# An output store that waits for an accumulating transfer, and a product split around another, in a convolution and two-matmul kernel

## The chip, the cores and the metric

The kernel runs on one core of a Trainium2 chip. The metric is the device time of one execution in microseconds (us); lower is better. The engines are called PE (TensorE, matmul), PEld (its weight loads), DVE (VectorE), ACT (ScalarE), POOL (GpSimd) and SP (SyncE, which here only issues DMAs). They run side by side, each in its own order, and wait for one another through semaphores.

## The reference

```python
w = weight_gen - max(weight_gen, axis=-1)          # (8, 4096, 8 heads, 7 taps)
w = exp(w);  w = w / (sum(w, axis=-1) + 1e-9)
x_pad = concatenate([zeros(B, 6, D), x], axis=1)   # six rows of zeros ahead of each batch row
x_unf = x_pad[:, arange(S)[:, None] + arange(7)]   # the seven rows that end at a token
y = einsum('bshk,bskhg->bshg', w, x_unf)           # (32768 tokens, 192), 24 channels per head
h = y @ w_in                                       # (192, 2048)
out = (h - tanh(h)) @ w_out                        # (2048, 192), float32
```

A convolution over seven taps whose weights are a softmax of their own for each token and head, and then two matmuls with `h - tanh(h)` between them.

## The kernel before

**Tiling.** The 32768 tokens are worked in 32 superblocks of 1024 tokens, numbered by `n`; each of the 128 partitions holds 8 tokens of a superblock (`J = 8`). A batch row is 4 superblocks long, so superblocks 0, 4, 8, ... begin with six rows of zeros, their halo.

**One superblock, stage by stage.**

1. SP loads `x` into one of four places of `x_ring` (line 172) and, for a superblock that begins a batch row, fills the halo with zeros (line 182). An even superblock's load brings its halo along (1344 KB), an odd one's shares it with the even one before (768 KB). SP also loads the weights `wg_t` (line 161, 224 KB).
2. ACT takes their exponential (line 202), DVE sums and scales it (`wsm`).
3. POOL multiplies `x` with the weights, tap by tap (line 297): taps 0 to 3 into the tile `pa`, taps 4 to 6 into `pb`. `pa` has three buffers, `pb` one. DVE makes one or two of the eight tokens of taps 0 to 2 (`HELP`); its operand stands at line 338.
4. POOL issues two accumulating DMAs (line 286). The three-tap transfer adds `pb` to taps 0 to 2 of `pa` (`first_sum`, in the profile `pa<-pb`, 1152 KB). For superblocks 10 to 31 the two-tap transfer (`second_sum`, `pa<-pa`, 768 KB) then adds taps 2 and 3 to taps 0 and 1, so that two taps are left to be added by PE; superblocks 4 to 9 leave four.
5. PE transposes what is left and adds it up in PSUM (`pc`, line 524), ACT copies it to `convT` (line 550).
6. In 16 steps `f`, PE makes 128 rows of `h` (`ph`, line 584), ACT their tanh (line 597), DVE the difference `gt` (line 598). In between PE runs the second matmul of the superblock before (`obank`, line 653), ACT copies its result to `out_sb` (line 672, two buffers), and SP stores it (line 676, 768 KB).

**Order.** The loop over `n` (its turns are called iterations here) writes out by hand what each step holds, and the order in which instructions are written is the order on each engine's queue. In iteration `n` PE works on the first matmul of superblock `n`. At step 1 the program writes, in this order: POOL's products of taps 0 to 3 of superblock `n + 2`, the two-tap transfer of `n + 1`, the load of `x` for `n + 3` (from iteration 9 on; it waits for the first of those products), and, after the second matmul's share of that step, the store of superblock `n - 2`. At a later step come POOL's product of taps 4 to 6 for `n + 2` and its three-tap transfer (`rest`), at step 8 the zero fill for `n + 3` where there is one, at step 11 the load of `wg_t` for `n + 5`, at steps 13 and 14 the transposes of `n + 1`. POOL and SP work strictly in this order: an instruction that waits holds up all behind it.

**Names that the change touches.** `LAST_TAP` and `FILL`: for the superblocks in `LAST_TAP`, tap 3 (which the three-tap transfer does not touch) is not made together with taps 0 to 2 but in `rest`: the first `FILL[n]` tokens just ahead of the three-tap transfer's issue, the others behind it. `LOCKED` and `LOCK`: for the superblocks in `LOCKED`, `rest` is written at step 10 and the three-tap transfer also waits for DVE's difference of that step. `dma_sum` returns the DMA instruction, `order(inst, other, reason)` makes one instruction wait for another (for a DMA: until it has landed).

Of the kernel before, what the change touches and what calls it, by code (L numbers as in the profile page):

```python
# [16 lines left out]
def kernel(  # L17
# [8 lines left out]
    nc = tc.nc  # L26
# [25 lines left out]
    EXTRA_NORM = False  # L52

    WG_AT = 11
    LOCK, LOCKED = 10, tuple(range(15, 32))
    WARM = 0
    SUM_LATE = ()
    SUM_BEHIND = ()
    HELP = {4: ((2, 3, 2, 1),), 5: ((3, 3, 2, 1),), 6: ((4, 3, 2, 1),), 7: ((5, 3, 2, 1),), 8: ((6, 3, 2, 1), (6, 12, 2, 1)), 9: ((7, 3, 2, 1), (7, 12, 2, 1)), 10: ((8, 3, 2, 1),), 11: ((9, 3, 2, 1),), 12: ((10, 3, 2, 1),), 13: ((11, 3, 2, 1),), 14: ((12, 3, 2),), 15: ((13, 3, 2),), 16: ((14, 3, 2),), 17: ((15, 3, 2),), 18: ((16, 3, 2),), 19: ((17, 3, 2),), 20: ((18, 3, 2),), 21: ((19, 3, 2),), 22: ((20, 3, 2),), 23: ((21, 3, 2),), 24: ((22, 3, 2),), 25: ((23, 3, 2),), 26: ((24, 3, 2),), 27: ((25, 3, 2),), 28: ((26, 3, 2),), 29: ((27, 3, 2),), 30: ((28, 3, 2),), 31: ((29, 3, 2),)}
    CUTS0 = [0, 2, 4]  # L60
    LAST_TAP = (4, 5, 6, 7, 8)
    X_LATE = ()
    ZERO_AT = 8
    PACE, PACED = None, ()
    SCALE_TWICE = True
    RELIEF = ()
    ACT_HELP = {}
    FILL = {4: 2, 5: 2, 6: 2, 7: 2, 8: 2}
    PART_FILL = {2: 1}
    SCALE_EARLY = ()  # L70
    REST2 = None
# [6 lines left out]
    X3_AT = 3  # L78
    X3_BEHIND = None
    HALF = ()  # L80
    WOUT_CAST = ()
    SKEW = 6
    TAPS1 = ((True, 0, 1, 0, 8), (True, 1, 2, 0, 8), (False, 4, 6, 0, 8), (False, 6, 7, 0, 8), (False, 2, 4, 0, 8))
# [56 lines left out]
    tap_of = {}  # L140
    pace_of = {}
    sum_of = {}

    def order(inst, other, reason):
        tc.add_manual_dep(
            inst.ins,
            other.ins.name,
            mybir.DependencyInfo(mybir.DependencyClass.Sync, mybir.DependencyReason.DATA),
            reason=reason,
        )  # L150
# [3 lines left out]
    def tokens(t, n):  # L154

        m = n // 2
        return t[2 * m * TOK : 2 * (m + 1) * TOK].rearrange("(p s j) ... -> p s j ...", p=P, j=J)[:, n % 2]
# [127 lines left out]
    def dma_sum(out, in_):  # L285
        return nc.gpsimd.dma_start(  # L286
            out=out.rearrange("p k j d -> p k (j d)"),
            in_=in_.rearrange("p k j d -> p k (j d)"),
            accum_op=mybir.AluOpType.add,
            max_dma_last_dim=2 * J * D,  # L290
        )
# [19 lines left out]
    def shares(n):  # L311

        top = [J] * KA
        dve, act = [], []
        for a, b, kh, nt in [(*e, 1)[:4] for e in HELP.get(n, ())]:
            dve.append((a, b, kh, top[0] - nt, top[0]))
            top[:kh] = [t - nt for t in top[:kh]]
        for a, b, k in ACT_HELP.get(n, ()):
            top[k] -= 1
            act.append((a, b, k, top[k]))  # L320
        return dve, act, top
# [35 lines left out]
    def products(n, taps=None, sums=None, hooks={}):  # L357
# [24 lines left out]
        def mul(eng, k0, k1, j0=0, j1=J):  # L382
            w = wsm_v if eng is nc.vector else wsm[:]
            return tap_product(eng, prod(k0, k1), x_t, w[:, j0:j1, :, k0:k1], (1, K), k0, k1, j0, j1)

        def parts(*ks):
            return [[prod(k, k + 1)[:, 0] for k in ks]] * NC
# [14 lines left out]

        end = KA - 1 if n in LAST_TAP else KA
        left = shares(n)[2]

        def most(k0, k1):
            return mul(nc.gpsimd, k0, k1, 0, left[k0])
# [7 lines left out]
        for k0, k1 in zip(cuts, cuts[1:]):  # L415
            if n - 1 in SUM2_EARLY and k0 == end - 1:
                second_sum(n - 1)
            m = most(k0, k1)
            if first is None and n - 1 in sum_of:
                sum_of.pop(n - 1)()  # L420
            first = first or m
        x_after[n + 1] = first
        second_sum(n - 1)
        def rest():
            a = PART_FILL.get(n, 0)
# [14 lines left out]
            else:  # L440
# [4 lines left out]

                if n in LAST_TAP and n in SUM_BEHIND:
                    most(KA - 1, KA)
# [3 lines left out]
                else:  # L451
                    a = min(FILL.get(n, 0), left[KA - 1]) if n in LAST_TAP else 0
                    if a:
                        mul(nc.gpsimd, KA - 1, KA, 0, a)
                    first_sum()
                    if n + 1 in SCALE_EARLY:
                        prescale(n + 1)
                    if n in LAST_TAP and a < left[KA - 1]:
                        mul(nc.gpsimd, KA - 1, KA, a, left[KA - 1])
                if n in TWO_SUMS:  # L460
                    to_sum[n] = pa
                    prods_of[n] = parts(0, 1)
                elif n in HALF:
                    to_sum[n] = pa
# [3 lines left out]
                if n == NTOT - 1:  # L468
                    second_sum(n)
                    third_sum(n)  # L470
# [3 lines left out]
    def prescale(n):  # L474

        wsm, wsm_v, e_t, zr = wsm_of[n]
        scale(nc.gpsimd, wsm[:], e_t, zr[:])
        wsm_of[n] = (wsm, wsm_v, None, None)

    def second_sum(n):  # L480

        if n in to_sum:
            pa = to_sum.pop(n)
            pairs = 1 if n in HALF else 2
            dma_sum(pa[:, 0:pairs], pa[:, 2 : 2 + pairs])
            if n in THREE or n in SINGLE:
                whole[n] = pa

# [150 lines left out]
    def out_stream():  # L639

        for i in range(LAST + 1):
            ops = []
            for r, blk in ((0, i), (1, i - 1)):
                if not 0 <= blk < LAST:
                    continue
                n, j = divmod(blk, J)
                if r == 0:
                    half[blk] = obank[blk % 2]
                ops.append((r, n, j, half[blk]))
            for f in range(NFT):  # L650
                for r, n, j, po in ops:
                    col = (j % 2) * HT + (j // 2) * P
                    mm = nc.tensor.matmul(  # L653
                        po[:, 0:D],
                        lhsT=g_of[n][f][r * R : (r + 1) * R, col : col + P],
                        rhs=w_out[r * R : (r + 1) * R, f, :],
                        start=(r == 0 and f == 0),
                        stop=(r == 1 and f == NFT - 1),
                    )
                    if r == 1 and f == 0 and i in (1, LAST):  # L660
                        order(mm, probe[0] if i == 1 else last_act[0], "row tiles in one bank")
                if f == NFT - 1 and i > 0:
                    store_out(i - 1)
                yield

    def store_out(blk):
        n, j = divmod(blk, J)
        po = half.pop(blk)
        if j == 0:
            out_of[n] = opool.tile([P, J, D], FP32, name="out_sb")  # L670
        out_sb = out_of[n]
        last_act[0] = nc.scalar.activation(out=out_sb[:, j, :], in_=po[:, 0:D], func=ACT.Copy)  # L672
        if j == J - 1:
            out_of.pop(n)
            g_of.pop(n)
            nc.sync.dma_start(
                out=tokens(out, n),
                in_=out_sb[:],
            )

    pairs = out_stream()

# [132 lines left out]
    if SOFT_EARLY:  # L815
# [6 lines left out]
        sums=SUMS1,  # L822
        hooks={} if WOUT_CAST else {6: load_w_out},
    )
# [202 lines left out]
```

## Time and profile before

| what | us |
|---|---|
| three runs | 738.18, 738.52, 741.08 (median 738.52) |
| the profiled execution's own time | 740.38 |
| its span in the profile | 738.5 |

| engine | busy us | instructions |
|---|---|---|
| PE | 716.7 | 13472 |
| DVE | 681.1 | 718 |
| POOL | 660.6 | 170 |
| ACT | 636.7 | 871 |

The profile records one execution. The chain of waits is the work that ended last, followed back from the end: at each step to what released it, or to the instruction before it on the same engine. A row of the timeline gives start, duration, engine, line, operation, the tiles, how many were merged, and in brackets how long the engine stood idle just before and what ended that. For DMAs the trace gives the issue on the queue that issues it (SPq, or POOL) and, where something waits for it, the time from issue to landing. Rows by line give count and shortest, median and longest duration in ns, with first and last start in us.

### The profile page before, as it was taken

Reading aid. Unit: us, or ns where it says so; the run is one execution under the profiler, and the core shown is the slowest. Engines: PE = TensorE matmul, PEld = TensorE weight load, DVE = VectorE, ACT = ScalarE, POOL = GpSimd, SP = SyncE. Lnnn points to the kernel's source line nnn. Section 1 sums busy time; section 2 is a strip of 40 time slices with the busy share of each in tenths; the row PEclk is TensorE's granted clock in tenths of the full one; section 3 lists DMA queues with packets and bytes.
Section 4 is the critical chain, followed back from the end, with each engine's and each line's share of the span. In section 5 each row is a group of like instructions: output and inputs, shape, how many; then the busy total and the mean of one; then the engine's idle time right before and its main releaser. Section 6 shows DMA issues by size and latency. Waiting matters only on the chain.

```text
span 738.5 us, 29769 instructions
## 1 busy us (share of the span) xinstructions
PE 716.7 (97%) x13472; PEld 551.1 (75%) x13472; DVE 681.1 (92%) x718; ACT 636.7 (86%) x871; POOL 660.6 (89%) x170
## 2 busy tenths in 40 slices
PE   3799999999998999999999999999999999999998
PEld 2477777777776777777777777777777777777777
DVE  7999999999998899999999999999999999988883
ACT  4888888988887889988989989898998999888882
POOL 7999999999999999989999999999999999996000
PEclk9999999999999999999999999999999999999999
DMA  7745276765558887766987878798786889766312
GB/s 203 163 101 162 101 188 142 184 177 122 136 145 206 199 227 168 175 158 171 233 206 172 191 147 206 179 236 197 157 185 160 207 197 216 172 140 110 88 45 87
DMA packets 35053, 122.97 MB, mean 167 GB/s; under 512 B 4607, under 2 KB 9455, under 8 KB 33006
## 3 DMA queue, kind: packets, MB, share of 16 engines
q0 software_dynamic: 20208, 53.48, 41.7%
q1 hardware_dynamic: 14718, 67.59, 26.1%
q8 instruction: 105, 1.72, 0.9%
q14 instruction: 22, 0.18, 0.1%
HBM read 45.08 MB, written 25.17 MB: 95 GB/s over the span
## 4 chain that ended last, share of the span: by engine, by line
PE 88%; DVE 4%; POOL 4%; DMA 2%; issue 1%; ACT 1%; POOLq 0%; DVEq 0%
PE obank L653 42%; PE ph L584 41%; PE pc L524 4%; POOL pa L297 2%; DVE gt L598 2%; PE po L697 1%; DMA pa<-pa 1%; POOL pb L297 1%; DVE pa L297 1%; DVE pb L297 0%; DMA wg_t<-in_weight_gen_dram 0%; ACT th L597 0%; POOL pa L286 0%; DVE obank L256 0%; DVE zsum L216 0%
## 5 line engine op out<-in xcount | busy, mean ns | idle before, releaser
L598 DVE TENSOR_TENSOR gt<-ph,th 128x1024 bf16<-128x1024 f32 x512 | 598.6, 1218 | 36.5 <-ACT th L597 29.7
L597 ACT ACTIVATE th<-ph 128x1024 f32<-128x1024 f32 x512 | 513.0, 1027 | 67.0 <-PE ph L584 52.8
L584 PE MATMUL ph<-convT,w_in 64*128 64x512 bf16 x3072 | 413.5, 378 | 4.6 <-DVE gt L598 3.6
L653 PEld LDWEIGHTS <-gt 64*128 64x128 bf16 x7936 | 354.0, 94 | 84.3 <-issue 12.4
L653 PE MATMUL obank<-w_out,gt 64*128 64x192 bf16 x7936 | 407.2, 243 | 0.1
L297 POOL TENSOR_TENSOR pa<-x_ring,wsm 128x3072 bf16<-128x3072 f32 (+2 forms) x73 | 346.1, 5008 | 0.2
L297 POOL TENSOR_TENSOR pb<-x_ring,wsm 128x4608 bf16<-128x4608 f32 (+4 forms) x34 | 286.3, 8423 | 2.2 <-DVE wsm L279 1.2
L584 PEld LDWEIGHTS <-w_in 64*128 64x128 bf16 x3072 | 159.8, 94 | 80.1 <-issue 12.8
L672 ACT ACTIVATE out_sb<-obank 128x192 f32<-128x192 f32 x248 | 81.7, 329 | 9.5 <-PE obank L653 8.3
L550 ACT ACTIVATE convT<-pc 128x1024 bf16<-128x1024 f32 (+1 forms) x62 | 50.7, 820 | 5.9 <-PE pc L524 5.6
L286 POOL DMA_DIRECT2D pa<-pa x24 | 39.5, 1648 | 8.3 <-DMA pa<-pb 8.0
L286 POOL DMA_DIRECT2D pa<-pb x28 | 37.3, 1333 | 10.4 <-POOL pb L297 6.7
L524 PEld LDWEIGHTS <-pa 64*128 64x128 bf16 x1920 | 39.2, 100 | 9.3 <-POOL pb L297 3.0
L524 PE MATMUL pc<-ident,pa 64*128 64x64 bf16 x1824 | 38.6, 191 | 4.1 <-DMA pa<-pa 2.5
L216 DVE TENSOR_REDUCE zsum<-wg_t 128x32 f32<-128x224 f32 (+1 forms) x61 | 23.6, 388 | 3.0 <-ACT wg_t L202 3.0
L202 ACT ACTIVATE wg_t<-wg_t 128x448 f32<-128x448 f32 x32 | 18.2, 569 | 6.8 <-DMA wg_t<-in_weight_gen_dram 6.8
L279 DVE TENSOR_TENSOR wsm<-wg_t,pc 128x448 f32<-128x448 f32 x27 | 16.8, 621 | 2.5
L297 DVE TENSOR_TENSOR pa<-x_ring,ph 128x384 bf16<-128x384 f32 x30 | 16.6, 554 | 1.3
L243 DVE RECIPROCAL pc<-zsum 128x64 f32<-128x64 f32 x27 | 14.8, 549 | 0.0
L524 PE MATMUL pc<-ident,pb 64*128 64x64 bf16 x216 | 4.9, 206 | 9.3 <-POOL pb L297 9.3
L524 PEld LDWEIGHTS <-pb 64*128 64x128 bf16 x288 | 6.3, 107 | 9.8 <-POOL pb L297 9.3
L697 PE MATMUL po<-w_out,gt 64*128 64x192 bf16 x256 | 11.9, 243 | 0.0
(26 smaller groups left out, 55.1 us busy)
## 6 DMA issues: line engine op xcount, KB each, us to landing
pa<-pb POOLq DMA_DIRECT2D x28, 1152.0 KB, 9.7
out_dram<-out_sb SPq DMA_DIRECT2D x31, 768.0 KB, 4.1
x_ring<-in_x_dram SPq DMA_DIRECT2D x15, 1344.0 KB, 8.3
pa<-pa POOLq DMA_DIRECT2D x24, 768.0 KB, 8.4
x_ring<-in_x_dram SPq DMA_DIRECT2D x17, 768.0 KB, 5.3
wg_t<-in_weight_gen_dram SPq DMA_DIRECT2D x32, 224.0 KB, 6.0
w_out<-in_moe_w_out_dram POOLq DMA_DIRECT2D x1, 768.0 KB, 9.7
out_dram<-out_sb SPq DMA_DIRECT2D x4, 192.0 KB, 3.5
```

Of the source, the lines that this page charges most:

```text
L202: last_exp[0] = nc.scalar.activation(out=wg_t[:].rearrange("p j h k -> p (j h k)"), in_=wg_t[:].rearrange("p j h k -> p (j h k)"), func=AC ...
L216: nc.vector.reduce_sum(out=zsum_of[n][:, j0 * H : j1 * H], in_=e_of[n][:, j0:j1].rearrange("p j h k -> p (j h) k"), axis=AX.X,)
L286: return nc.gpsimd.dma_start(out=out.rearrange("p k j d -> p k (j d)"), in_=in_.rearrange("p k j d -> p k (j d)"), accum_op=mybir.AluOpTyp ...
L297: return eng.tensor_mul(bass.AP(tensor=out.tensor, offset=out.offset + j0 * D, ap=[out.ap[0], [J * D, nk], [G, run], [1, G]]), bass.AP(ten ...
L524: nc.tensor.matmul(pc[r][:, col : col + R] if home else pc[:, r, col : col + R], lhsT=prods[c][gi][r * R : (r + 1) * R, 2 * j : 2 * j + 2] ...
L550: last_conv[0] = nc.scalar.activation(out=out, in_=pc[:, :, 0:cols].rearrange("p r (cj t) -> p r cj t", t=R), func=ACT.Copy,)
L584: nc.tensor.matmul(ph[:, r, :], lhsT=w_in[r * R : (r + 1) * R, c, ff], rhs=convT[r * R : (r + 1) * R, c, :], start=(c == 0), stop=(c == NC ...
L597: last_act[0] = nc.scalar.activation(out=th[:], in_=ph_f, func=ACT.Tanh)
L598: last_sub[0] = nc.vector.tensor_sub(gt[:], ph_f, th[:])
L653: mm = nc.tensor.matmul(po[:, 0:D], lhsT=g_of[n][f][r * R : (r + 1) * R, col : col + P], rhs=w_out[r * R : (r + 1) * R, f, :], start=(r == ...
L672: last_act[0] = nc.scalar.activation(out=out_sb[:, j, :], in_=po[:, 0:D], func=ACT.Copy)
L697: nc.tensor.matmul(po[:, r, 0:D], lhsT=g_of[n][f][r * R : (r + 1) * R, col : col + P], rhs=w_out[r * R : (r + 1) * R, f, :], start=(f == 0 ...
```

## The change

Three tables grow and one wait is added. Superblock 14 joins `LOCKED`. Superblocks 9 and 10 join `LAST_TAP` and `FILL`, with two tokens ahead of the transfer. And the store of superblock `n` (5 to 30, where superblock `n + 3` has a two-tap transfer that is already written, so 7 to 28) waits until the two-tap transfer of `n + 3` has landed; that transfer is written in the same step just ahead of the store.

```diff
-    LOCK, LOCKED = 10, tuple(range(15, 32))
+    LOCK, LOCKED = 10, tuple(range(14, 32))
...
-    LAST_TAP = (4, 5, 6, 7, 8)
+    LAST_TAP = (4, 5, 6, 7, 8, 9, 10)
...
-    FILL = {4: 2, 5: 2, 6: 2, 7: 2, 8: 2}
+    FILL = {4: 2, 5: 2, 6: 2, 7: 2, 8: 2, 9: 2, 10: 2}
...
+    STORE_BEHIND = tuple(range(5, 31))
...
+    second = {}
...
             pa = to_sum.pop(n)
             pairs = 1 if n in HALF else 2
-            dma_sum(pa[:, 0:pairs], pa[:, 2 : 2 + pairs])
+            second[n] = dma_sum(pa[:, 0:pairs], pa[:, 2 : 2 + pairs])
...
-            nc.sync.dma_start(
+            dma = nc.sync.dma_start(
                 out=tokens(out, n),
                 in_=out_sb[:],
             )
+            if n in STORE_BEHIND and n + 3 in second:
+                order(dma, second[n + 3], "order of the transfers")
```

Each engine runs the same instructions in the same order as before, except that on POOL, for superblocks 9 and 10, one product of 128x3072 becomes three of 128x1536, 128x384 and 128x1152; the last of them stands behind the three-tap transfer.

## The prediction

> I write F1(n) for the three-tap transfer of superblock n (line 286, `pa<-pb`) and S2(n) for its two-tap transfer (`pa<-pa`).
>
> **What bounds the kernel now.** I read the page first, then busy time by superblock, then the chain of waits, then single lines around the one place that stood out.
>
> ```profile
> PE 716.7 (97%) x13472; PEld 551.1 (75%) x13472; DVE 681.1 (92%) x718; ACT 636.7 (86%) x871; POOL 660.6 (89%) x170
> ```
>
> TensorE is busy 97%. An average hides where the other 3% lie, so I cut the span at superblocks (columns: window, length, busy time of PE, PEld, DVE, ACT, POOL, granted clock, DMA share, GB/s):
>
> ```profile
> 177.00:199.50 22.50, 22.50 (x450) 17.20 (x448) 21.54 (x25) 19.92 (x28) 22.20 (x6) 1.00 0.63 166
> 222.50:248.10 25.60, 23.08 (x397) 17.62 (x394) 20.44 (x23) 19.53 (x28) 25.30 (x6) 0.93 0.89 212
> 270.05:291.82 21.77, 21.77 (x402) 16.77 (x400) 20.85 (x23) 19.65 (x28) 21.47 (x6) 1.00 0.80 197
> 235.60:238.55 2.95, 0.43 (x31) 0.44 (x30) 2.34 (x3) 1.02 (x1) 2.65 (x3) 1.00 0.14 40
> 238.55:241.95 3.40, 3.40 (x49) 2.69 (x43) 0.00 (x0) 1.49 (x2) 3.40 (x2) 0.50 0.83 145
> ```
>
> Before iteration 9 a superblock takes 22.50 us with TensorE full (450 matmuls); after it 21.77, full again (402). There only less matmul work would help. Iteration 9 alone takes 25.60, of which 3.83 (25.60 - 21.77) is loss: TensorE stands, and then has half its clock for 3.40 us. All that this change can win is in that window. The chain, in order of time (start, us, what), says who is late:
>
> ```profile
> 192.76 0.57 DVE pa L297
> 193.33 0.03 POOLq L286
> ...
> 217.10 9.48 POOL pa L297 x2
> ...
> 227.11 10.90 DMA pa<-pa
> ```
>
> S2(10) was issued by POOL at 227.11, after products of its own, and took 10.90. The row of the matmuls that waited for it (the transposes of superblock 10, `pc`), and POOL's and SP's rows around it, from the timeline:
>
> ```profile
> 238.14 0.74 PE L524 MATMUL pc<-ident,pa 64*128 64x64 bf16 x32 [2.52 <-DMA pa<-pa]
> ...
> 110.56 1.76 POOL L286 DMA_DIRECT2D pa<-pb  x1
> 130.92 1.76 POOL L286 DMA_DIRECT2D pa<-pb  x1
> 174.30 2.71 POOL L297 TENSOR_TENSOR pa<-x_ring,wsm 128x1152 bf16<-128x1152 f32 x1
> 180.70 6.09 POOL L297 TENSOR_TENSOR pa<-x_ring,wsm 128x3072 bf16<-128x3072 f32 x1
> 186.28 8.80 POOL L297 TENSOR_TENSOR pb<-x_ring,wsm 128x4608 bf16<-128x4608 f32 x1
> 195.38 1.29 POOL L286 DMA_DIRECT2D pa<-pb  x1 [0.30 <-POOL pb L297]
> 215.82 1.28 POOL L286 DMA_DIRECT2D pa<-pb  x1 [0.30 <-POOL pb L297]
> 227.11 1.72 POOL L286 DMA_DIRECT2D pa<-pa  x1
> 237.50 1.28 POOL L286 DMA_DIRECT2D pa<-pb  x1 [0.30 <-POOL pb L297]
> 238.32 11.01 POOL L297 TENSOR_TENSOR pa<-x_ring,wsm 128x2688 bf16<-128x2688 f32 x2
> 248.79 1.72 POOL L286 DMA_DIRECT2D pa<-pa  x1
> 270.47 1.72 POOL L286 DMA_DIRECT2D pa<-pa  x1
> 326.33 1.28 POOL L286 DMA_DIRECT2D pa<-pb  x1 [2.39 <-DVE gt L598]
> ...
> 222.10 0.33 SPq L172 DMA_DIRECT2D x_ring<-in_x_dram  x1
> 222.53 1.25 SPq L676 DMA_DIRECT2D out_dram<-out_sb  x1
> 232.07 0.70 SPq L182 DMA_DIRECT2D x_ring<-zero  x1
> 232.87 0.62 SPq L161 DMA_DIRECT2D wg_t<-in_weight_gen_dram  x1
> ```
>
> The stall is 2.52, so TensorE wanted S2(10) at 235.62 (238.14 - 2.52). The rest of the 3.83, 1.31, is the halved clock.
>
> [...]
>
> **Tap 3 split for 9 and 10 (FILL, LAST_TAP).** Taps 2 and 3 (128x3072, 5.58 from 180.70 to 186.28) become 128x1536, 128x384 and, behind F1, 128x1152. Superblocks that already do this show F1 to F1 in 20.36 (110.56 to 130.92), those that do not 20.44 (195.38 to 215.82): the pieces cost nothing, because the 384 runs in the 0.30 that F1 waits for `pb` anyway. F1(9) would be ready at 180.70 + 2.8 (half of 5.58) + 9.1 (186.28 to 195.38) = 192.6; but VectorE's help product for 9 releases line 286 only at 193.36 (193.33 + 0.03 in the chain), so F1(9) goes at 193.4, 2.0 early. F1(10) follows at 213.3 to 213.8 (20.36, or less by the 0.5 that POOL idled). Then S2(10) = F1(10) + 11.29 (215.82 to 227.11) + the 1152 left over (2.7 by its row, some 0.5 of it under its neighbours, as 6.09 is 5.58 from start to start for the larger product) = 226.8 to 227.8. Before: 227.11. All of POOL's work still stands ahead of S2(10), so this part alone is worth -0.3 to +0.7; I take 0. What it does buy is that F1(10) leaves the DMA engines 2 us sooner.
>
> **The store behind S2.** In SP's order stand: load of x(12), store of block 7, zero fill of x(12)'s halo, load of wg. The store (768 KB) now goes only once S2(10) has landed. What S2 takes in other company:
>
> ```profile
> L286 POOL DMA_DIRECT2D pa<-pa x1: 1722/1722/1722, 270.5 to 270.5; - x1
> ...
> DMA to landing us min/median/max: 8.8/8.8/8.8
> L286 POOL DMA_DIRECT2D pa<-pa x1: 1715/1715/1715, 248.8 to 248.8; - x1
> ...
> DMA to landing us min/median/max: 8.3/8.3/8.3
> L286 POOL DMA_DIRECT2D pa<-pa x1: 1213/1213/1213, 684.0 to 684.0; - x1
> ...
> DMA to landing us min/median/max: 7.0/7.0/7.0
> ```
>
> With no load of x beside it 7.0 (S2(31)); with the large load of x, and a store issued just before it, 8.8 (S2(12)); here 10.9 with the store 4.6 ahead of it (222.53). No row has the large load without a store. Bounds 7.0 and 10.9; I take 8.0, below 8.8 because store, zero fill and wg (232.87, inside S2's time) all go. S2(10) then lands at 227.1 + 8.0 = 235.1, 0.5 before TensorE wants it. Stall and halved clock go: -3.83, less 0.2 for a rest of the stall: **-3.6**.
>
> What is queued behind the store pays for it. The zero fill now comes after it, and POOL's first product of superblock 12 (238.32, that is S2 + 11.2) needs it. Its own landing no row shows; the nearest is the store's:
>
> ```profile
> wg_t<-in_weight_gen_dram SPq DMA_DIRECT2D x32, 224.0 KB, 6.0
> pa<-pb POOLq DMA_DIRECT2D x28, 1152.0 KB, 9.7
> ...
> L676 SPq DMA_DIRECT2D out_dram<-out_sb x31: 332/344/1272, 66.4 to 725.3; - x31
> ...
> DMA to landing us min/median/max: 3.4/4.1/7.6
> ```
>
> The store is issued at S2 + 8.1 and alone lands in 3.4. A zero fill that ends with it is in place at S2 + 11.5: POOL waits 0.3. If it first begins when the store has landed, and takes another 3.4, POOL waits 3.7. Below, 0. I take 0.3, since it is issued 0.4 after the store and is 4.5 KB. It happens for superblocks 12, 16, 20, 24 and 28.
>
> [...]
>
> Does TensorE feel a late POOL? It wants S2(11) one superblock after 235.62, at 257.4. S2(11) is issued at 248.8 + 0.3 and, with the smaller load of x and no store, takes at most 8.3: lands at 257.4, more likely 256.6. From there POOL repeats in 21.68 (248.79 to 270.47) against TensorE's 21.77, and is 2.39 ahead of its lock at 326.33. So waits of 0.3 every fourth superblock (POOL regains 4 x 0.09 between) stay covered.
>
> The wg load would go at 235.1 + 0.1 + 0.4 + 0.7 = 236.3 and land at 242.3 (6.0); its exponential on ScalarE ran at 247.3, 243.5 after the gain. Covered by 1.2 here, more later.
>
> ```profile
> L202 ACT ACTIVATE wg_t<-wg_t x1: 570/570/570, 247.3 to 247.3; 128x448 f32<-128x448 f32 x1
> ```
>
> If wg were late, ScalarE would stand in line with its tanh behind it. The output buffer comes around only after two superblocks: a store 8 us later costs nothing. F1 goes 10.4 after S2 (227.11 to 237.50) and meets the store's last 1.1; it has 11.29 against its 9.7: covered by 1.6.
>
> **Lock for 14.** F1(14) now waits for VectorE's subtraction at step 10 of iteration 12, one superblock before the 326.3 of F1(15): 304.5, and 300.9 after the gain. POOL comes to F1(14) at about 302.6 (237.50 + 3 x 21.68), later: no wait, 0.
>
> **Sum.** -3.6 against the profiled execution's 740.38 (span 738.5 and 1.9 around it) gives 736.8. The median of the three runs, 738.52, lies 1.86 lower, so **734.9** for the median. The three runs spread by 2.9, about what this stall with its clock is worth, so runs may have had it in part.
>
> **Rivals.**
> A. S2(10) stays a little late (9.5 instead of 8.0): stall 1.0, clock perhaps kept. Gain 2.5: 736.0. For it: 8.8 was with a store only just ahead.
> B. The change does nothing: another stream (the large x load) held S2(10), which still lands at 10.9; the stall stays at 2.5, and FILL gives -0.3 to +0.7: 738.5. For it: S2(12) beside the large load takes no less than 8.8. Against: DMA share falls to 0.14 while TensorE waits, after 16 us of transfers close together that the store was part of.
> C. The zero fill takes the store's place as the wait, five times. At 2.0 each, less the 0.36 regained: 5 x 2.0 - 4 x 0.36 = 8.6 of delay in POOL. TensorE absorbs what POOL is ahead: 2.4 at the lock, and about 1.5 from faster transfers. 8.6 - 3.9 - 3.6 = +1.1: 739.6; at 2.6 each +4.1: 742.6. It turns the sign from about 1.8 each. Against: in 3.4 us even the whole store is through.
> D. The store, now released just ahead of every F1, makes F1 longer than the 11.29 that S2 leaves it. At 12.5 POOL waits 1.2 for some 20 superblocks, 24, less 3.9 and 3.6: 755. Against: only 1.1 of overlap.
>
> **How the numbers follow.** Forecast 0.55, A 0.15, B 0.08, C 0.17, D 0.05. The likeliest gives 734.9. Half a per cent, about what a measurement of this kernel can tell from no change, is 3.7 us: below 734.8 is faster, above 742.2 slower. The forecast lies on that edge: of its 0.55 I give 0.38 to faster and 0.17 to same; A goes to same but for 0.02; B to same; C is half same, half slower; D slower. Faster 0.40, same 0.46, slower 0.14. The low end, 733.8, is the whole 3.83 and a runs' scatter of about 0.9; the high end, 739.8, takes in A, B and the milder half of C. Forecast's own range: 733.8 to 736.0.
>
> **What would show it.** The step from 222.50 on takes 21.8 to 22.5 and not 25.6, with the clock at 1.00 and no wait of `pc` for `pa<-pa`. S2(10) is issued within 0.7 of 227.1 and lands in 8.5 or less. The store of block 7 is issued at 234 to 236 instead of 222.53. F1(9) goes at 193.4. POOL's product for 12 shows a wait under 0.5 for a transfer. I am wrong if S2(10) still lands after 235.6, if POOL waits over 1.5 for the zero fill, or if F1 lands later than 11.3 after its issue.

## The result and the profile after

| | runs | median us | lowest to highest |
|---|---|---|---|
| before | 15 | 738.97 | 737.75 to 741.23 |
| changed | 15 | 737.07 | 735.85 to 740.14 |

The ratio is 0.9974 with a 95% interval of 0.9963 to 0.9986: faster by 1.9 us (0.26%), where 3.6 had been forecast. The profiled execution of the changed kernel took 736.08 (span 734.2), against 740.38 (span 738.5) before: 4.3 us less. So one pair of profiles shows more than the forecast, and the medians show half of it. The profile of before lies 1.4 above its median of 738.97, that of the changed kernel 1.0 below its own. The experiments had to explain that difference.

The shares of the chain of waits by engine in the kernel before, then the engines' busy times and the same shares in the changed kernel:

```profile
PE 88%; DVE 4%; POOL 4%; DMA 2%; issue 1%; ACT 1%; POOLq 0%; DVEq 0%
...
PE 714.7 (97%) x13472; PEld 549.7 (75%) x13472; DVE 681.0 (93%) x718; ACT 636.4 (87%) x871; POOL 661.0 (90%) x174
...
PE 94%; DVE 4%; ACT 0%; DMA 0%; issue 0%; DVEq 0%
```

TensorE now holds 94% of the chain instead of 88%, and POOL is no longer in it. Busy time of iteration 9 in the changed kernel, first cut at its new length and then at the length it had before (columns as in the prediction):

```profile
222.50:244.30 21.80, 21.80 (x407) 16.85 (x403) 20.91 (x23) 19.68 (x28) 21.50 (x7) 1.00 0.74 186
222.50:248.10 25.60, 25.60 (x480) 20.06 (x476) 24.63 (x29) 23.16 (x32) 25.30 (x7) 1.00 0.78 195
```

The superblock takes 21.8 with TensorE full, and the clock stays at 1.00. In the 25.60 us in which before 397 matmuls ran, 480 run. The timeline of the changed kernel around that place: TensorE's transposes of superblock 10, POOL from F1(9) on, and SP:

```profile
235.55 0.65 PE L526 MATMUL pc<-ident,pa 64*128 64x64 bf16 x32
...
193.97 1.29 POOL L288 DMA_DIRECT2D pa<-pb  x1 [0.81 <-POOL pa L299]
213.85 1.76 POOL L288 DMA_DIRECT2D pa<-pb  x1
227.32 2.19 POOL L288 DMA_DIRECT2D pa<-pa  x1
228.10 9.79 POOL L299 TENSOR_TENSOR pb<-x_ring,wsm 128x4608 bf16<-128x4608 f32 x1
238.19 1.28 POOL L288 DMA_DIRECT2D pa<-pb  x1 [0.30 <-DMA x_ring<-zero]
...
222.79 0.33 SPq L174 DMA_DIRECT2D x_ring<-in_x_dram  x1
234.86 0.34 SPq L678 DMA_DIRECT2D out_dram<-out_sb  x1
235.29 0.70 SPq L184 DMA_DIRECT2D x_ring<-zero  x1
236.10 0.91 SPq L163 DMA_DIRECT2D wg_t<-in_weight_gen_dram  x1
```

The transposes begin at 235.55 with no wait in brackets. S2(10) is issued at 227.32 (before: 227.11); the store of block 7 has gone from 222.53 to 234.86, which is when S2(10) has landed. The two-tap transfers of superblocks 10 and 12 by themselves:

```profile
L288 POOL DMA_DIRECT2D pa<-pa x1: 2195/2195/2195, 227.3 to 227.3; - x1
...
DMA to landing us min/median/max: 7.5/7.5/7.5
...
L288 POOL DMA_DIRECT2D pa<-pa x1: 1717/1717/1717, 271.2 to 271.2; - x1
...
DMA to landing us min/median/max: 7.3/7.3/7.3
```

S2(10) takes 7.5 instead of 10.9, S2(12) 7.3 instead of 8.8. The packets in the traces show what gave way: before, the store's packets (6144 bytes each) ran from 228.7 to 234.3, among those of S2(10), the last of which ended at 237.7; in the changed kernel S2(10)'s ended at 234.5 and the store's began at 235.7. The signs that the prediction named for this place came, but for F1(9), which went at 193.97 and not at 193.4.

### The profile page after: what moved, and what is told of

It is laid out like the page before. It is cut to its first block, busy times and chain, and to the rows that moved or that the text cites. A ratio compares the mean times of both kernels' runs of the same rounds, so it can differ in the third digit from the quotient of the medians.

```text
span 734.2 us, 29779 instructions
## 1 busy us (share of the span) xinstructions
PE 714.7 (97%) x13472; PEld 549.7 (75%) x13472; DVE 681.0 (93%) x718; ACT 636.4 (87%) x871; POOL 661.0 (90%) x174
## 3 DMA queue, kind: packets, MB, share of 16 engines
q8 instruction: 105, 1.72, 0.9%
## 4 chain that ended last, share of the span: by engine, by line
PE 94%; DVE 4%; ACT 0%; DMA 0%; issue 0%; DVEq 0%
PE obank L655 45%; PE ph L586 44%; PE pc L526 4%; DVE gt L600 2%; PE po L701 1%; DVE pa L299 1%; DVE pb L299 0%; DMA wg_t<-in_weight_gen_dram 0%; DVE obank L258 0%; DVE zsum L218 0%; DVE wsm L281 0%; ACT th L599 0%; ACT wg_t L204 0%; DVE obank L281 0%; ACT convT L544 0%
```

## The experiments

All ratios are against the kernel before, run on the same chip.

| kernel | runs | median us | ratio | 95% interval |
|---|---|---|---|---|
| before again | 12 | 739.27 | 1.0009 | 0.9997 to 1.0022 |
| changed again | 5 | 736.30 | 0.9969 | 0.9957 to 0.9981 |
| store's wait alone | 7 | 736.68 | 0.9963 | 0.9946 to 0.9981 |
| tap 3's split alone | 11 | 739.09 | 1.0006 | 0.9997 to 1.0014 |
| lock of 14 alone | 12 | 739.17 | 0.9998 | 0.9988 to 1.0008 |
| only block 7's store waits | 11 | 739.76 | 1.0007 | 0.9997 to 1.0016 |
| only blocks 8 to 28 wait | 12 | 737.70 | 0.9980 | 0.9970 to 0.9989 |
| store behind zero fill and wg | 7 | 736.75 | 0.9971 | 0.9959 to 0.9982 |

**The kernel before, three more profiles.** No edit.

> The kernel before, once more, for the spread of its runs. Theory 1 (the stall of iteration 9 differs from run to run in how much of the 3.83 us it takes, because the transfer's time and the place of the 3.4 us clock window differ): the times spread over 2.5 to 3.5 us, and this profile shows the wait of the transposes of superblock 10 at another size than 2.52 us (0.5 to 2.5), with or without half the clock after it. Theory 2 (the stall is the same in every run, and the change loses elsewhere what the first profile of after does not show): the wait is again within 0.3 us of 2.52, with half the clock behind it.

> The kernel before, a third profile. Theory 1: the wait at superblock 10 is between 1.0 and 2.6 us; where it is under about 2 us the clock stays at 1.00 and the execution is within 1 us of 738.7; where it is over 2 us, half the clock for 3.4 us follows and the execution is over 740.

> The kernel before, a fourth profile. Theory 1, as for the third: a wait at superblock 10 of 1.0 to 2.6 us, with half the clock behind it only where it is over about 2 us, and a time over 740 only there.

The 3.4 us clock window of these expectations can be seen in the traces: the clock records change in steps of 3.413 us (last section). The wait at superblock 10 and the clock right after it, by timeline and by window. First the second profile of before (738.29 us), then the third (740.24), then the fourth (738.41):

```profile
237.61 0.65 PE L524 MATMUL pc<-ident,pa 64*128 64x64 bf16 x32 [1.65 <-DMA pa<-pa]
238.30:241.70 3.40, 3.40 (x80) 2.82 (x76) 1.04 (x1) 3.12 (x5) 3.40 (x2) 1.00 0.55 96
```

```profile
238.27 1.04 PE L524 MATMUL pc<-ident,pa 64*128 64x64 bf16 x32 [2.44 <-DVE gt L598]
238.30:241.70 3.40, 3.40 (x58) 2.69 (x60) 0.00 (x0) 1.02 (x1) 3.40 (x2) 0.52 0.75 129
```

```profile
237.93 0.65 PE L524 MATMUL pc<-ident,pa 64*128 64x64 bf16 x32 [2.21 <-DMA pa<-pa]
238.30:241.70 3.40, 3.40 (x91) 2.82 (x85) 0.72 (x1) 2.80 (x5) 3.40 (x2) 1.00 0.75 130
```

The wait is there each time, at 1.65, 2.44 and 2.21, and half the clock follows in one of the three. (In the third profile the brackets name VectorE. S2(10) took 11.0 there and landed at 238.2, just ahead of the 238.27: it is the same wait, and the name in brackets is only the last event seen.) Of the four profiled executions of before, the two with half the clock, 740.38 and 740.24, are the two over 740; the two without, 738.29 and 738.41, lie 0.6 to 0.7 below the median of 738.97. The profile that the prediction was made from was one of the dear ones: 4 of the 15 runs of before are over 740. That half the clock follows where the wait is over about 2 us, as was expected, does not hold: the fourth profile has 2.21 without it, and the lock of 14 alone 2.71 without it:

```profile
239.18 0.65 PE L526 MATMUL pc<-ident,pa 64*128 64x64 bf16 x32 [2.71 <-DMA pa<-pa]
238.30:241.70 3.40, 2.52 (x76) 2.26 (x78) 0.49 (x1) 1.55 (x2) 3.33 (x2) 1.00 0.49 87
```

**The changed kernel again.** No edit.

> The changed kernel, once more. Theory 1: a span near 734 to 735.5 and no wait of TensorE after 100 us longer than 0.5 us in this profile. Theory 2 (the two-tap transfers land only 0.4 to 1.7 us ahead of TensorE, so that many runs have a late one): a span of 735.5 to 737, with a wait of pc for pa<-pa somewhere behind iteration 9.

Span 734.2, TensorE full in iteration 9 at clock 1.00, no wait for a two-tap transfer at all: theory 1. Theory 2, a loss of the changed kernel that its first profile did not show, found nothing in this one profile.

**The store's wait alone.** Against the changed kernel:

```diff
-    LAST_TAP = (4, 5, 6, 7, 8, 9, 10)
+    LAST_TAP = (4, 5, 6, 7, 8)
...
-    FILL = {4: 2, 5: 2, 6: 2, 7: 2, 8: 2, 9: 2, 10: 2}
+    FILL = {4: 2, 5: 2, 6: 2, 7: 2, 8: 2}
...
-    LOCK, LOCKED = 10, tuple(range(14, 32))
+    LOCK, LOCKED = 10, tuple(range(15, 32))
```

> The store's wait alone; LAST_TAP, FILL and LOCKED as before. If the store's place does the work (theory 1): two-tap transfer of superblock 10 issued at 227.1, landing in 7.2 to 8.0, stall under 0.3; ratio within 0.001 of the full change's. If tap 3's split is what counts: stall over 1.5 us, ratio 0.999 to 1.001.

S2(10) in this kernel, and the transposes:

```profile
L288 POOL DMA_DIRECT2D pa<-pa x1: 1722/1722/1722, 228.3 to 228.3; - x1
...
DMA to landing us min/median/max: 7.3/7.3/7.3
...
236.52 0.65 PE L526 MATMUL pc<-ident,pa 64*128 64x64 bf16 x32
```

7.3 and no wait, and a ratio of 0.9963 against 0.9969 beside the same runs of the kernel before for the full change. Within these intervals the store does all of it. The profiled execution (737.08) is the slowest of its seven runs: TensorE comes to the transposes 1.0 later than in the changed kernel (236.52 against 235.55) without having waited for a two-tap transfer, which is taken up below.

**Tap 3's split alone.** `STORE_BEHIND = ()` and the old `LOCKED`.

> Tap 3's split for 9 and 10 alone (and nothing else). Theory 1: the two-tap transfer of superblock 10 is issued at 227.3 and still takes 9.5 to 10.9, the stall stays at 1.5 to 2.7 us; ratio 0.999 to 1.001. If the three-tap transfer's leaving 2 us sooner is enough: it lands in under 8.5, no stall, ratio below 0.998.

```profile
L288 POOL DMA_DIRECT2D pa<-pa x1: 2189/2189/2189, 227.8 to 227.8; - x1
...
DMA to landing us min/median/max: 10.0/10.0/10.0
...
237.98 0.65 PE L526 MATMUL pc<-ident,pa 64*128 64x64 bf16 x32 [1.77 <-DMA pa<-pa]
```

S2(10) still takes 10.0 and TensorE waits 1.77: the split is worth nothing by itself, ratio 1.0006. It is not free for POOL, though. S2(10)'s issue takes 2.19 there instead of the 1.72 of the kernels without the split, and F1(11) goes 10.87 after S2(10) (227.80 to 238.67), where with the store's wait alone it goes 10.41 after it (228.30 to 238.71).

**The lock of 14 alone.** `STORE_BEHIND = ()` and the old `LAST_TAP` and `FILL`.

> Superblock 14 in LOCKED and nothing else of the change. As costed: the three-tap transfer of superblock 14 waits up to 2.1 us for VectorE and that of 15 correspondingly less, its two-tap transfer lands about as far ahead of TensorE as its neighbours' (over 1 us), TensorE waits nowhere new: ratio 0.999 to 1.001. If a later POOL costs there: ratio above 1.001, with a wait of pc for pa<-pa at superblock 14 or 15.

Ratio 0.9998. The wait at superblock 10 is there (2.71, above), and TensorE waits nowhere new.

**Only block 7's store waits.** Against the changed kernel:

```diff
-    STORE_BEHIND = tuple(range(5, 31))
+    STORE_BEHIND = (7,)
```

> The change with only the store of block 7 waiting; the stores of blocks 8 to 28 go as before. Theory 1a (iteration 9 is the only place): ratio as for the full change, 0.996 to 0.998. Theory 1b (the later two-tap transfers, 9 to 10 us beside a large load of x and a store, land only 0.4 to 0.9 us ahead of TensorE in the second profile of before, so a TensorE that is 1.6 us earlier runs into the next of them): the wait of pc for pa<-pa goes from superblock 10 to superblock 12 or 16, about 1 us long, and the ratio is 0.9985 to 0.9998.

The transposes of superblocks 11 and 12 in this kernel, and S2(12):

```profile
258.14 0.65 PE L526 MATMUL pc<-ident,pa 64*128 64x64 bf16 x32 [0.59 <-DMA pa<-pa]
...
281.25 0.65 PE L526 MATMUL pc<-ident,pa 64*128 64x64 bf16 x32 [1.10 <-DVE gt L600]
...
L288 POOL DMA_DIRECT2D pa<-pa x1: 1715/1715/1715, 271.2 to 271.2; - x1
...
DMA to landing us min/median/max: 10.0/10.0/10.0
```

Superblock 10 no longer waits, but 11 waits 0.59 and 12 waits 1.10 (S2(12) lands at 281.2; with its store moved it takes 7.3), together 1.7, and the ratio is 1.0007. Theory 1b: the stall was handed on. Iteration 9 is where the loss showed, not the only place that causes it. The ratio is a little above the 0.9985 to 0.9998 that theory 1b named, and the profiled execution (738.18) is the fastest of its 11 runs; what the median, 1.6 higher, loses besides was in no profile.

**Only blocks 8 to 28 wait.** `STORE_BEHIND = tuple(range(8, 31))`, all else as changed; three profiles.

> The full change without the wait of block 7's store; the stores of blocks 8 to 28 wait. Theory 1b (both are needed: block 7's wait ends the stall at superblock 10, the later ones keep TensorE from meeting the next late transfer): the transfer of superblock 10 takes 9 to 10.9 again and TensorE waits 1.5 to 2.5 us for it; behind it the two-tap transfers land 2.5 us or more ahead of TensorE; ratio 0.999 to 1.001. If the later stores gain by themselves: ratio under 0.998.

> A second profile of the change without block 7's wait (its first profile fell on the slowest of its 12 runs). Theory 3 (TensorE's loss is the largest lateness over all two-tap transfers, not their sum: with the later stores behind, only superblock 10 can be late): the time lies 0.3 to 2.5 us over the full change's 736.1 to 737.1 by just the wait of pc at superblock 10, and no other wait of pc for pa<-pa is found. If the wait at superblock 10 is 1.5 us or more while the time is under 737.5, theory 3 is wrong.

> A third profile of the change without block 7's wait. Theory 3, as for the second: time = full change's 736.1 to 737.1 plus the wait of pc at superblock 10 (plus about 1.4 us where half the clock follows it), and no other wait of pc for pa<-pa.

The expectation of 0.999 to 1.001 was wrong: 0.9980, between the two kernels. The transposes of superblock 10 in the three profiles (738.79, 737.78 and 737.35 us):

```profile
238.41 0.65 PE L526 MATMUL pc<-ident,pa 64*128 64x64 bf16 x32 [1.85 <-DMA pa<-pa]
```

```profile
237.20 0.65 PE L526 MATMUL pc<-ident,pa 64*128 64x64 bf16 x32 [0.61 <-DMA pa<-pa]
```

```profile
236.76 0.65 PE L526 MATMUL pc<-ident,pa 64*128 64x64 bf16 x32 [1.16 <-DVE zsum L218]
```

(In the third the brackets name VectorE again; S2(10) landed there at 236.6, just ahead.) No other transposes wait for a two-tap transfer. Time less wait is 736.9, 737.2 and 736.2: theory 3, a loss that is the largest lateness of all two-tap transfers and not their sum. A TensorE that has waited for one transfer comes later to the next, so that waits which follow one another (0.59 and 1.10 with block 7 alone) are steps of one lateness. In the second profile of before, S2(12) was issued at 271.1, took 10.4 and landed at 281.5. That is 2.2 after the changed kernel begins the transposes of superblock 12 (279.27), but that TensorE, already 1.65 late, began them at 281.60 and did not wait.

Time less wait fits the others too: 738.41 - 2.21 = 736.2 and 738.29 - 1.65 = 736.6 for before, 738.87 - 1.77 = 737.1 for the split alone, 739.68 - 2.71 = 737.0 for the lock alone, 738.18 - 1.69 = 736.5 for block 7 alone; for the two profiles with half the clock another 1.3 goes off: 736.6 and 736.5. With no wait the times are 736.08 (the changed kernel, twice), 736.53 and 737.08.

What is left of the spread, 736.1 to 737.1, is for the most part older than iteration 9. The start of superblock 10's transposes less the wait before them is when TensorE was ready for S2(10): 235.55 in the changed kernel, 236.52 with the store's wait alone, 236.56, 236.59 and 235.60 in the three profiles here, which are of one kernel. When what is over 235.55 is taken off as well, all fourteen profiles lie between 735.9 and 736.5. So an execution can lose up to 1.0 ahead of the stall, whatever the change does; why it does was not tried.

The wait itself varies with the transfer: S2(10) took 10.1, 8.9 and 9.4 in these three, and TensorE was ready 8.4 after its issue in each. Why it took less here than in most profiles of before was not tried either.

**The store behind the zero fill and wg.** The waiting store is kept in a list at step 1 and issued at step 11:

```diff
             if f == WG_AT:
                 weights(n)
+                while later:
+                    later.pop(0)()
```

> The full change, with the waiting store written behind the zero fill and the load of wg (step 11) instead of ahead of them, so that nothing of iteration 9 is queued behind it. If the zero fill behind the store costs POOL 0.5 us in iteration 9 and nothing later: the three-tap transfer of superblock 11 is issued 10.4 after the two-tap transfer of 10 instead of 10.9, the two-tap transfer of 10 takes up to 0.7 us longer (wg and zero fill beside it), and the time is the same within 0.001. If the zero fill's place matters more than that: ratio lower than the full change's by 0.001 or more.

POOL in this kernel, from S2(10) to S2(11):

```profile
227.78 2.19 POOL L289 DMA_DIRECT2D pa<-pa  x1
228.56 9.79 POOL L300 TENSOR_TENSOR pb<-x_ring,wsm 128x4608 bf16<-128x4608 f32 x1
238.64 1.28 POOL L289 DMA_DIRECT2D pa<-pb  x1 [0.30 <-POOL pb L300]
```

The expected 10.4 from S2(10) to F1(11) did not come: it is 10.86, as in the changed kernel (10.87), although the zero fill now goes well ahead. In both, F1(11) is POOL's product of 9.79 plus 0.30. So the zero fill cost nothing even where it was named in brackets (238.19 in the changed kernel): it happened to land then. The 0.5 more than in the kernel before is the split's, which has 10.87 by itself. The ratio is that of the change.

This run also answers whether it is the store or what stands behind it on SP's queue (zero fill and wg) that has to stay away from S2(10). Here both are issued beside S2(10), at 229.43 and 230.23, and only the store waits; S2(10) takes 8.0 and TensorE does not wait for it. So moving the store is enough; the 8.0 against 7.5 leaves about 0.5 for the other two, by one profile each.

## Why the prediction was half right

1. *All that can be won lies in iteration 9.* Right as to where the loss shows, wrong as to what holds the gain: with block 7's store alone the stall moved on to superblocks 11 and 12. The prediction put no price on the later stores. The change holds them back as well, so this error did not show in the time; that is luck.
2. *Tap 3's split is worth 0.* Right in time: S2(10) at 227.32 against 227.11, ratio 1.0006. F1(9) went at 193.97 instead of the 193.4 forecast. That the pieces cost nothing was not right: the step from S2(10) to F1(11) grew by 0.5 with them, which TensorE did not feel.
3. *S2(10) takes 8.0 with the store behind it.* Right, a little better: 7.5.
4. *Stall and halved clock go: -3.83, less 0.2.* **This step failed, in size.** The 3.83 was one execution's loss. The wait was 2.52 there and 2.44, 2.21 and 1.65 in three others, and half the clock, priced at 1.31, came in two of the four. The sum was made in the profiled execution and then carried over to the median unchanged, though the prediction had seen that the median lay 1.86 lower and the runs spread by about the size of this stall. The mechanism held (S2(10) in 7.5, no wait, the clock at 1.00); the size did not. In the executions at 738.3 and 738.4 only a wait of 1.65 to 2.21 is to be had, and 1.9 was measured between the medians. The forecast of 734.9 lies under the fastest of the 15 runs of the changed kernel (735.85). The changed kernel's own median, 737.07, lies 1.0 over its profiles; the profiles of other kernels show up to 1.0 lost ahead of iteration 9, but no run of the changed kernel near its median is among the profiles, so for these runs that is not shown.
5. *The zero fill costs POOL 0.3, five times.* No cost was found: moving the store behind it left the step from S2(10) to F1(11) at 10.9 and the time as it was. The prediction let the zero fill end with the store; in the changed kernel its six packets of 768 bytes ended at 237.9, the store's last at 238.6.
6. *The lock of 14 costs 0.* Right: 0.9998.
7. *Rivals.* A (a stall that stays) and B (nothing happens) did not occur: S2(10) lands in time. C and D (the zero fill, a longer F1) did not either: POOL's only wait named for the zero fill is the 0.3 above, and F1 takes 9.6 in the median, where it took 9.7. TensorE is full in iteration 9 and in the superblocks behind it (529.97 us of the 530 from 200 to 730).

## What to carry to other kernels

A transfer on the path of the busiest engine was made shorter here by holding back one that nobody was waiting for (S2(10), 10.9 to 7.5). What that was worth was the largest lateness of any transfer of its kind, so look at all of them: with only one of the stores held back, the next late transfers took the gain (waits of 0.59 and 1.10, ratio 1.0007). Before a stall is priced from one profile, set the profiled execution's own time beside the median: if it lies above, part of the stall may belong to that execution alone, and the term for the median is smaller by as much. A name in brackets is the last event before the start, not yet the cause: taking the named thing away is the test (with the zero fill well ahead, POOL's 0.30 stayed).

## What the runs showed of the hardware

- Half the clock after a stall is not a matter of the stall's length alone: stalls of 2.52 and 2.44 had it for about 3.4 us (granted clock 0.50 and 0.52), stalls of 2.71 and 2.21 did not (1.00). In the profiles of before and of the changed kernel the clock records change only within 0.02 of whole multiples of 3.413 us from the first one: in that of before, 0.50 begins 66.01 such steps after it (238.55) and ends at 67.01 (241.97). Cut along such steps, TensorE was busy for 0.89 and 1.12 in the step just ahead of the two halved ones. In the two longest stalls of iteration 9 that kept the clock (2.71, the lock alone, and 2.21, the fourth profile of before) the idle time was shared between two steps, and the emptier one was busy for 1.64 and 1.53:

```profile
235.14:238.55 3.41, 0.89 (x35) 0.44 (x30) 2.80 (x4) 1.31 (x3) 3.11 (x3) 1.00 0.23 70
...
234.71:238.13 3.42, 1.12 (x18) 0.53 (x12) 3.42 (x4) 1.96 (x3) 3.12 (x2) 1.00 0.39 105
...
237.40:240.82 3.42, 1.64 (x54) 1.48 (x56) 1.39 (x2) 1.08 (x2) 3.12 (x3) 1.00 0.25 48
...
236.05:239.46 3.41, 1.53 (x52) 1.40 (x54) 1.99 (x3) 1.57 (x2) 3.11 (x3) 1.00 0.10 23
```

  So half the clock came after steps in which TensorE was idle for 2.52 and 2.30 of 3.4 us, and did not come after 1.78 and 1.88. No run shifted a stall on purpose, so whether a limit lies between them is not shown.
- The same accumulating transfer of 768 KB, S2(10), took 7.5 (the changed kernel) and 7.3 (the store's wait alone) where block 7's store and what is queued behind it were held back, 8.0 where the store alone was, and 9.7 to 11.1 in the kernels of the table where no store waits.
